# One fused attention and mixture-of-experts kernel: last tiles' ranks from one-hots, an early overflow count, row gathers ahead of weights, an expert's first product in three parts, and a planner's TensorE durations renewed

## The chip, the cores and the metric

The kernel runs on one core of a Trainium2 chip. The metric is the device time of one execution in microseconds (us). The engines are TensorE (PE in the rows; PEld is its loading of stationary operands), VectorE (DVE), ScalarE (ACT), GpSimd (POOL) and SyncE (SP). SP issues most transfers, GpSimd the indirect ones.

## What is computed

```python
# attention: 4 batches, 8 heads, 768 positions of 64, plus 8 memory positions; chunks of 32
for c in range(nc):
    k_full = np.concatenate([mem_k, k_ctx], axis=2)      # 16 left, 32 own, 8 right
    scores = scale * np.matmul(q_c, k_full.transpose(0, 1, 3, 2))
    a = softmax(scores)                                  # + 1e-9 in the denominator
    out[:, :, c_start:c_end] = np.matmul(a, v_full)
# first FFN: 3072 tokens x 512, hidden 2048
h = x @ w_in
x = (h * np.cos(h)) @ w_out
# top-1 of 8 experts (512 -> 1024 -> 512); tokens with x @ w_skip <= 0 keep x
logits = xc @ w_gate
e_idx = np.argmax(logits, axis=1)
h = np.maximum(xc[mask] @ w1[e], 0.0)
y[mask] = gate_w[mask, None] * (h @ w2[e])               # gate_w: the softmax at e_idx
out[do_compute] = xc + y
```

## The kernel before

Every float32 operand of a large product is split into a high and a low part, and a product is the sum of three passes (high by high, high by low, low by high). So one h of a unit is 12 matmuls and one y is 3.

**Stages.** Attention runs over 24 tiles (tile c is chunk c's 32 positions in all four batches, 128 tokens). Two tiles make a group g; the first FFN has 16 pieces of the hidden size, so 192 units (g, f), each with one h (L580, function `plan_unit`), the chain for h cos h on ScalarE and VectorE (L608 to L619), and two y groups (L584). Attention for later tiles lies between the units of earlier ones, so the first FFN begins at 22 us while its weights are still being loaded and unpacked (L546 to L559). A tile whose y is done gets its gate logits: for most tiles on VectorE (L687), for the last two (the tail) as matmuls on TensorE (L782 and L794). `plan_gates` then makes a one-hot of the chosen expert (`onehot`, L716), a rank in the expert's region (`base` L726 and L727: the running count of all tiles before, then `rank` L730 with a triangular matrix), adds the one-hot to the running count (`count`, L722), picks this row's rank (`mine`, L735), adds the offset (`index`, L740) and writes the rows to DRAM at these places (`scatter`, L743, an indirect transfer). A scatter waits until the one before it has landed.

**Experts.** The first expert is named before the tail. After the tail `plan_caps` counts tokens per expert (L844), orders the other seven by size (L848 to L860), and SP loads their seven numbers into registers (L863). From then on SP loads rows of the regions (`plan_rows`, L959, tile xg) and weight pieces (`plan_piece32`, L929, tile raw; converted to w by L238 and L938). The gathers of rows read what the scatters wrote, so they wait for the last scatter. Most experts take `plan_unit2` over two tiles at a time; the first expert and the two small ones (third and seventh in the order) take `plan_pair`, one tile with a quarter of the hidden size: h (L1042, 12 matmuls), relu on ScalarE (L1047), two transposes ("turn", L1052), the split into gh and gl (L238, L1059), two groups of y (L996, 3 matmuls each). `plan_finish` joins (L1084) and puts rows into the output by an indirect transfer (L1088). At the end TensorE counts once more (L1262), VectorE compares with the capacity (L1265 to L1267), all five engines load the result into a register (L1269) and branch on it (L1270); nothing overflows here.

**What sets the order.** A planner on the host (`Schedule`) simulates the engines: each task has an engine, a duration, a key and what it waits for, and whenever an engine comes free it takes the ready task with the smallest key. The instructions are then written in the order the simulation found, and each engine runs its own list strictly in that order. Durations given to the planner thus set the order and nothing else. SP's list is in one order too: a load that waits holds up all loads behind it.

## Time and profile before

| | us |
|---|---|
| runs shown | 853.3, 852.24 (and one of 1259.52) |
| median | 853.3 |
| the profiled execution's own time | 850.34 |
| its span | 848.2 |
| TensorE busy in the span | 820.9 (97%) |
| VectorE, ScalarE, GpSimd busy | 589.9, 525.1, 252.7 |
| granted TensorE clock, mean | 0.995 |

The span runs from the first to the last instruction; 2.1 us of the execution lie around it. Times in rows are us from the span's start. Matmuls are pipelined and their ends are modelled, so that a stretch in which TensorE is shown busy may still hold less work than it could; the start of the next row shows more than a row's length. In the rows of a timeline the bracket at the end gives the idle time before the instruction and what ended it.

### The profile page before, as it was taken

How to read it: one execution, taken by the hardware profiler on the slowest of the kernel's cores; microseconds unless marked ns; L12 is line 12 of the kernel's file. 1: busy time of each engine (PE TensorE's matmuls, PEld its weight loads, DVE VectorE, ACT ScalarE, POOL GpSimd, SP SyncE). 2: the span in 40 equal slices, each digit the busy share in tenths (PEclk: the TensorE clock that was granted, in tenths of full speed). 3: DMA queues.
4: the chain of work that ended last, by engine and by line, in shares of the span. 5: the costliest groups of instructions: out<-in, count | busy, mean ns of one | idle time of the engine just before them, and what ended most of it. 6: DMA issues, size and time to landing. Idle time of an engine off the chain costs nothing.

```text
span 848.2 us, 17771 instructions
## 1 busy us (share of the span) xinstructions
PE 820.9 (97%) x6440; PEld 710.8 (84%) x6440; DVE 589.9 (70%) x1598; ACT 525.1 (62%) x1204; POOL 252.7 (30%) x330
## 2 busy tenths in 40 slices
PE   9899899999999999999999999999999999999994
PEld 4677788778888888888888888888888789889993
DVE  7888874899649376493855839567398386697761
ACT  6887876556657566565665656556577375575551
POOL 6465453323323223232232322323233100010010
PEclk9999999999999999999999999999999999999998
DMA  9469527623123131221312213221213275886640
GB/s 351 165 193 251 179 101 250 182 69 101 44 74 91 33 100 33 85 74 33 100 54 76 71 34 100 65 63 28 104 30 122 86 268 205 277 294 207 204 175 30
DMA packets 37200, 106.08 MB, mean 125 GB/s; under 512 B 6747, under 2 KB 7003, under 8 KB 36976
## 3 DMA queue, kind: packets, MB, share of 16 engines
q1 hardware_dynamic: 34064, 98.74, 38.0%
q0 software_dynamic: 3040, 6.13, 2.0%
q8 instruction: 52, 0.85, 0.4%
q14 instruction: 44, 0.36, 0.1%
HBM read 88.10 MB, written 20.77 MB: 128 GB/s over the span
## 4 chain that ended last, share of the span: by engine, by line
PE 77%; DVE 8%; ACT 5%; issue 3%; DMA 3%; SPq 1%; POOL 1%; DVEq 0%; POOLq 0%; ACTq 0%
PE pb L580 34%; PE py L584 25%; PE py L996 8%; PE pb L448 4%; PE pb L1042 2%; DVE junk L687 2%; PE pb L380 2%; DMA st<-in_w_in_dram 1%; DVE pb L549 1%; DVE cv L555 1%; DVE u L619 1%; DVE ki L608 1%; PE pb L472 1%; DMA raw<-in_w_dram 1%; ACT w L238 1%
## 5 line engine op out<-in xcount | busy, mean ns | idle before, releaser
L580 PE MATMUL pb<-xh,w 128*128 128x256 f32 x1856 | 266.2, 286 | 4.7 <-DVE u L619 3.5
L580 PEld LDWEIGHTS pb<-xh,w 128*128 128x128 f32 x1856 | 246.3, 190 | 27.1 <-DVE u L619 7.0
L627 POOL TENSOR_TENSOR gl<-u,gh 128x256 fp32r<-128x256 f32 x192 | 147.3, 767 | 357.0 <-ACT gh L238 271.3
L584 PE MATMUL py<-w,gh 128*128 128x512 f32 x768 | 244.3, 399 | 0.6 <-ACT yt L238 0.3
L687 DVE SCALAR_TENSOR_TENSOR junk<-yt,wg 128x512 bf16<-128x512 f32 x198 | 149.2, 754 | 7.4 <-ACT yt L238 5.3
L584 PE MATMUL py<-w,gl 128*128 128x512 f32 x384 | 150.8, 393 | 0.8 <-POOL gl L627 0.7
L580 PE MATMUL pb<-xl,w 128*128 128x256 f32 x928 | 148.9, 283 | 0.0
L584 PEld LDWEIGHTS py<-w,gh 128*128 128x128 f32 x768 | 131.8, 190 | 20.3 <-ACT gh L238 1.7
L608 DVE SCALAR_TENSOR_TENSOR ki<-pb,ki 128x256 f32<-128x256 f32 x192 | 80.5, 419 | 82.7 <-ACT ki L238 82.4
L619 DVE SCALAR_TENSOR_TENSOR u<-ki,pb 128x256 f32<-128x256 f32 x192 | 80.0, 417 | 73.6 <-ACT ki L615 70.5
L580 PEld LDWEIGHTS pb<-xl,w 128*128 128x128 f32 x928 | 127.8, 191 | 0.0
L238 ACT ACTIVATE ki<-pb 128x256 int32<-128x256 f32 x192 | 72.9, 381 | 86.7 <-PE pb L580 67.5
L612 ACT ACTIVATE ki<-ki 128x256 f32<-128x256 f32 x192 | 79.7, 416 | 63.5 <-DVE ki L608 63.3
L238 ACT ACTIVATE gh<-u 128x256 fp32r<-128x256 f32 x192 | 79.5, 414 | 57.7 <-DVE u L619 51.0
L938 DVE TENSOR_TENSOR w<-raw,w 128x512 fp32r<-128x512 f32 x128 | 84.4, 693 | 11.8 <-ACT w L238 10.0
L584 PEld LDWEIGHTS py<-w,gl 128*128 128x128 f32 x384 | 72.1, 188 | 20.9 <-POOL gl L627 4.5
L615 ACT ACTIVATE ki<-ki 128x256 f32<-128x256 f32 x192 | 79.7, 415 | 4.7
L238 ACT ACTIVATE w<-raw 128x512 fp32r<-128x512 f32 x128 | 74.8, 625 | 10.4 <-DMA raw<-in_w_dram 9.7
L996 PE MATMUL py<-w,gh 128*128 128x512 f32 x224 | 72.1, 403 | 0.0
L1088 POOL DMA_INDIRECT out_dram<-ot,ri x14 | 14.9, 1062 | 151.9 <-DVE ot L1084 117.9
L559 POOL TENSOR_TENSOR w<-cv,w 128x512 fp32r<-128x512 f32 x32 | 41.3, 1294 | 27.6 <-ACT w L238 26.1
L996 PE MATMUL py<-w,gl 128*128 128x512 f32 x112 | 43.8, 391 | 0.0
(151 smaller groups left out, 840.5 us busy)
## 6 DMA issues: line engine op xcount, KB each, us to landing
raw<-in_w_dram SPq DMA_DIRECT2D x64, 512.0 KB, 4.5
k<-in_kt_dram SPq DMA_DIRECT2D x40, 256.0 KB, 4.9
v<-in_vw_dram SPq DMA_DIRECT2D x40, 256.0 KB, 4.1
st<-in_w_in_dram SPq DMA_DIRECT2D x16, 512.0 KB, 6.5
st<-in_w_out_dram SPq DMA_DIRECT2D x16, 512.0 KB, 3.6
out_dram<-yt SPq DMA_DIRECT2D x96, 64.0 KB, 1.8
q<-in_qt_dram SPq DMA_DIRECT2D x21, 256.0 KB, 2.9
xs<-fl SPq DMA_DIRECT2D x8, 528.0 KB, 11.2
```

The lines of the kernel that those rows point to most:

```text
L238: nc.scalar.activation(out=out, in_=in_, func=AF.Copy, scale=scale)
L559: nc.gpsimd.tensor_tensor(out=wt[f][:, i, 1, :], in0=o["f"], in1=wt[f][:, i, 0, :].bitcast(F32), op=ALU.subtract)
L580: nc.tensor.matmul(ph, w[:, i, ct, :], x[j][:, ct, :], start=(n == 0), stop=(n == len(todo) - 1))
L584: nc.tensor.matmul(py, g[i][:, t * P:t * P + P], w[:, j, :], start=(first and n == 0), stop=(last and n == 2))
L608: nc.vector.scalar_tensor_tensor(out=o["v"], in0=o["p"], scalar=INV2PI / W_SCALE, in1=o["k"], op0=ALU.mult, op1=ALU.subtract)
L612: nc.scalar.activation(out=o["v"], in_=o["v"], func=AF.Sin, scale=math.pi)
L615: nc.scalar.activation(out=o["v"], in_=o["v"], func=AF.Square, scale=math.sqrt(2.0))
L619: nc.vector.scalar_tensor_tensor(out=o["u"], in0=o["v"], scalar=1.0, in1=o["p"], op0=ALU.subtract, op1=ALU.mult)
L627: nc.gpsimd.tensor_tensor(out=o["g"][1], in0=o["u"], in1=o["g"][0].bitcast(F32), op=ALU.subtract)
L687: nc.vector.scalar_tensor_tensor(out=junk, in0=o["y"][:, 0:DM], scalar=1.0, in1=state["wg"][:, j, :], op0=ALU.mult, op1=ALU.mult, accum_ou ...
L938: nc.vector.tensor_tensor(out=part(s, 1), in0=half(s), in1=part(s, 0).bitcast(F32), op=ALU.subtract)
L996: nc.tensor.matmul(ey[p, t], g[i][:, cols], w[:, j, 512 * (f % 2):512 * (f % 2) + 512], start=(f == 0 and q == 0), stop=(f == n - 1 and q ...
```

## The change

1. The planner's durations of seven TensorE tasks are set anew: transposes of attention and splits 0.87 to 0.45, scores and weighted sums 0.95 to 0.69, the tail's transposes and dots to 0.45, h 1.32 to 1.44, y 0.66 to 0.69.
2. `plan_pair`: h is planned as three tasks of four matmuls, so that other TensorE work may stand between them.
3. The tail: the second tile's base takes the first one's one-hot as a matmul of its own, and the counts are three matmuls over the running count and the two one-hots. The two `count` additions of the tail are gone.
4. Row gathers have the key of their use less GK = 8, where it was less 2; weight pieces keep less 2.
5. The overflow number is worked out on VectorE right behind `caps` (`most`), from a copy of the counts. The matmul and four VectorE instructions at the end are gone; the load into registers stays.

```diff
+GK = 8
@@ plan_xt, plan_chunk, plan_tail_logits (the last two of these lines)
-        a = pe(0.87, key, pe_x, after + [xt], new=[b], use=use)
+        a = pe(0.45, key, pe_x, after + [xt], new=[b], use=use)
-        t = pe(0.95, key, scores, [lq] + lk + s0 + clean["k", z], new=[b1] + mine, use=[sq, sk] + bz(0) + bz(2) + hold)
+        t = pe(0.69, key, scores, [lq] + lk + s0 + clean["k", z], new=[b1] + mine, use=[sq, sk] + bz(0) + bz(2) + hold)
...
@@ plan_unit
-        t = pe(1.32, i - AHEAD * end, h, [w_ready["i", f]] + xt_ready[g], new=[b], use=[w_slot[f], xt_slot[g]])
+        t = pe(1.44, i - AHEAD * end, h, [w_ready["i", f]] + xt_ready[g], new=[b], use=[w_slot[f], xt_slot[g]])
...
@@ plan_gates
         def base():
             o["r"] = bank()[:, 0:E]
+            if tail:
+                end_hots.setdefault("sum", state["sum"])
+                end_hots[t] = o
             nc.tensor.matmul(o["r"], ones, first_slot, start=True, stop=False)
             nc.tensor.matmul(o["r"], ones, state["sum"], start=False, stop=False)
+            if tail and t:
+                nc.tensor.matmul(o["r"], ones, end_hots[0]["oh"], start=False, stop=False)
...
-        if c == NCH - 2:
-            before = [last["skip"]]
+        if tail:
+            before = [last["skip"]] + ([last["hot"]] if t else [])
...
-        n = dve(0.07, key + 0.01, count, [h, r])
+        if tail:
+            n = last["hot"] = r
+        else:
+            n = dve(0.07, key + 0.01, count, [h, r])
@@ plan_counts
-            nc.tensor.matmul(o["p"], ones, state["sum"], start=True, stop=True)
+            terms = [end_hots["sum"], end_hots[0]["oh"], end_hots[1]["oh"]] if first else [state["sum"]]
+            for n, x in enumerate(terms):
+                nc.tensor.matmul(o["p"], ones, x, start=(n == 0), stop=(n == len(terms) - 1))
...
             if first:
+                state["cnt"] = sm.tile([P, E], F32, name="cnt")
+                nc.vector.tensor_copy(out=state["cnt"], in_=o["p"])
@@ plan_caps
+        def most():
...
+            nc.vector.tensor_tensor(out=state["over"], in0=state["cnt"], in1=state["cp"], op=ALU.subtract)
+            nc.vector.reduce_max(out=top, in_=state["over"], axis=AX.X)
+            nc.vector.tensor_copy(out=state["top"], in_=top)
+
+        x = dve(0.07, key + 9, caps, [o["sort"]])
+        dve(0.25, key + 9.5, most, [x])
@@ plan_rows
-        x = load(key - 2, ld, P * ROW * 4, [last["reg", p]] + after, new=[s_xg])
+        x = load(key - GK, ld, P * ROW * 4, [last["reg", p]] + after, new=[s_xg])
@@ plan_pair
-        def h():
-            o["p"] = bank()[:, 0:G]
+        def h(third):
+            if not third:
+                o["p"] = bank()[:, 0:G]
...
-        x = pe(1.32, key, h, w2_ready[ma] + xt_ready["x", p][t:t + 1], new=[b1],
+        x = pe(0.48, key, lambda: h(0), w2_ready[ma] + xt_ready["x", p][t:t + 1], new=[b1],
                use=[w2_slot[ma], xt_slot["x", p]])
+        for third in (1, 2):
+            x = pe(0.48, key, lambda third=third: h(third), [x], use=[b1, w2_slot[ma], xt_slot["x", p]])
@@ the end
-    nc.tensor.matmul(pc, ones, state["sum"], start=True, stop=True)
-    nc.vector.tensor_copy(out=cnt, in_=pc)
...
-    nc.vector.tensor_copy(out=topi, in_=top)
     order_cm.__exit__(None, None, None)
-    most = nc.values_load(topi[0:1, 0:1], min_val=0, max_val=NT + P)
+    most = nc.values_load(state["top"][0:1, 0:1], min_val=0, max_val=NT + P)
```

**First place: TensorE at the beginning of the first FFN.** Before (names: k0, k1 and q0, more are keys and queries of a chunk, xh and xl the first group's input, w_112 the first weight piece):

```order
L315 MATMUL pb_405<-ones_83 64x512
L448 MATMUL py_409<-k0_96,q0_98 32x128 x16
L580 MATMUL pb_430<-xh_108,w_112 128x256 x8
L580 MATMUL pb_430<-xl_109,w_112 128x256 x4
L448 MATMUL py_453<-k1_101,more_103 32x128 x16
L580 MATMUL pb_476<-xh_108,w_113 128x256 x8
```

In the changed kernel, on the same engine at the same place (a row of L316 is a filler matmul, which no result uses):

```order
L316 MATMUL pb_398<-ones_83 64x512
L581 MATMUL pb_401<-xh_108,w_112 128x256 x8
L581 MATMUL pb_401<-xl_109,w_112 128x256 x4
L449 MATMUL py_418<-k0_96,q0_98 32x128 x16
L316 MATMUL pb_439<-ones_83 64x512
```

The first h now stands ahead of the scores that preceded it. From here to the row at which 180.6 us is reached in the profile, TensorE's list holds the same tasks in another order, less two fillers; the scores of the next two tiles, for one, stand one and two y groups earlier. From 180.6 to about 640 us the list is the same task by task.

**Second place: SP's queue and TensorE behind the scatters.** SP before, behind the seven register loads (only the transfers; the register arithmetic between them is left out):

```order
L959 DMA xg_9356<-xs_80 128x528
L929 DMA raw_9361<-in_w12_dram 128x1024
L929 DMA raw_9366<-in_w12_dram 128x1024
L959 DMA xg_9370<-xs_80 128x528
L959 DMA xg_9375<-xs_80 128x528
L929 DMA raw_9380<-in_w12_dram 128x1024
```

SP in the changed kernel:

```order
L981 DMA xg_9342<-xs_80 128x528
L981 DMA xg_9347<-xs_80 128x528
L981 DMA xg_9355<-xs_80 128x528
L951 DMA raw_9362<-in_w12_dram 128x1024
L951 DMA raw_9367<-in_w12_dram 128x1024
```

The three gathers stand together ahead of all weight pieces. Behind fourteen transfers stands SP's load of the overflow number, which was the last thing in its list. On TensorE the first split of gathered rows (L380) stood behind all four h of the first tile and seven of its eight y groups:

```order
L996 MATMUL py_9227<-w_8824,gl_9354 128x512
L380 MATMUL pb_9390<-cb_81,xg_9356 128x128 x4
L996 MATMUL py_9227<-w_8824,gh_9353 128x512 x2
L996 MATMUL py_9227<-w_8824,gl_9354 128x512
L1042 MATMUL pb_9409<-w_8523,xh_9021 128x256 x4
```

Now it stands behind four of the eight, and the next two splits follow with one y group between (L381 splits, L1018 y):

```order
L381 MATMUL pb_9380<-cb_81,xg_9342 128x128 x4
L1018 MATMUL py_9301<-w_8769,gh_9352 128x512 x2
L1018 MATMUL py_9301<-w_8769,gl_9353 128x512
L381 MATMUL pb_9408<-cb_81,xg_9347 128x128 x4
L1018 MATMUL py_9301<-w_8769,gh_9352 128x512 x2
L1018 MATMUL py_9301<-w_8769,gl_9353 128x512
L381 MATMUL pb_9428<-cb_81,xg_9355 128x128 x4
```

Three y groups moved from ahead of the first split to behind it, and the two fillers that stood ahead of it are gone from here.

**Third place: TensorE at the end.** Before, the last h (L1042), the last turn (L1052) and what stands behind:

```order
L1042 MATMUL pb_11310<-w_10944,xh_10942 128x256 x4
L996 MATMUL py_11292<-w_10872,gh_11296 128x512 x2
L996 MATMUL py_11292<-w_10872,gl_11297 128x512
L1052 MATMUL pb_11328<-cb_81,u_11326 128x128 x2
L996 MATMUL py_11292<-w_10872,gh_11296 128x512 x2
L996 MATMUL py_11292<-w_10872,gl_11297 128x512
L996 MATMUL py_11292<-w_10932,gh_11306 128x512 x2
```

Five y groups begin behind the turn (the last row here is the second of them); the first three do not need this turn. Now:

```order
L1018 MATMUL py_11288<-w_10939,gl_11320 128x512
L1066 MATMUL pb_11323<-w_10951,xh_10949 128x256 x4
L1076 MATMUL pb_11344<-cb_81,u_11342 128x128 x2
L1018 MATMUL py_11288<-w_11002,gh_11347 128x512 x2
L1018 MATMUL py_11288<-w_11002,gl_11348 128x512
L1018 MATMUL py_11288<-w_11002,gh_11347 128x512 x2
L1018 MATMUL py_11288<-w_11002,gl_11348 128x512
```

No y group stands between the last third of h and its turn, and only the two that need this turn stand behind it.

## Rows read from the trace of the kernel before

**Rows 1.** Windows view: stretch, length, busy us of PE, PEld, DVE, ACT, POOL; clock; DMA.

```profile
22.40:160.00 137.60, 130.30 (x1038) 109.37 (x1038) 104.79 (x208) 105.53 (x238) 68.80 (x77) 1.00 0.63 191
160.00:181.00 21.00, 18.21 (x169) 14.27 (x171) 20.83 (x74) 11.30 (x23) 5.94 (x8) 1.00 0.37 95
181.00:663.00 482.00, 481.10 (x3947) 424.46 (x3938) 325.81 (x994) 296.90 (x697) 146.16 (x211) 1.00 0.25 69
663.00:691.00 28.00, 25.84 (x171) 21.32 (x171) 16.70 (x65) 15.10 (x38) 2.97 (x3) 1.00 0.59 213
691.00:836.00 145.00, 144.96 (x935) 130.61 (x933) 102.68 (x225) 80.99 (x189) 12.92 (x12) 1.00 0.62 210
836.00:848.20 12.20, 0.22 (x2) 0.10 (x1) 1.30 (x5) 0.00 (x0) 0.98 (x1) 0.68 0.09 28
```

**Rows 2.** Lines view of TensorE in 22.4 to 180.6: busy, mean ns, idle before it.

```profile
L580 PE MATMUL pb<-xh,w 128*128 128x256 f32 x352 | 51.4, 289 | 4.7 <-DVE u L619 3.5 <-DVE cv L555 1.1
```

**Rows 3.** Timeline of TensorE around the first h: start, length, engine, line, instruction.

```profile
22.36 1.08 PE L448 MATMUL py<-k,q 128*32 128x128 f32 x32
23.38 0.85 PE L580 MATMUL pb<-xh,w 128*128 128x256 f32 x5
```

**Rows 4.** Timeline of SyncE's queue at 63 us, the loads of one chunk's keys.

```profile
63.35 1.11 SPq L417 DMA_DIRECT2D k<-in_kt_dram  x2
```

**Rows 5.** DMA view of 60 to 70 us: issues, KB each, median us to landing.

```profile
k<-in_kt_dram SPq DMA_DIRECT2D x2, 256.0 KB, 9.2
```

**Rows 6.** Timeline of TensorE, scores of that chunk.

```profile
81.20 1.08 PE L448 MATMUL pb<-k,more 128*32 128x128 f32 x32
```

**Rows 7.** Timeline of GpSimd, the two last scatters.

```profile
666.22 1.01 POOL L743 DMA_INDIRECT xs<-yt,si  x1 [6.94 <-ACT u L1047]
670.52 0.98 POOL L743 DMA_INDIRECT xs<-yt,si  x1 [3.29 <-DVE gl L1059]
```

**Rows 8.** Timeline of VectorE, the second scatter's row numbers.

```profile
667.17 0.16 DVE L740 TENSOR_TENSOR si<-sl,aw 128x1 int32<-128x1 f32 x1
```

**Rows 9.** Timeline of SyncE's queue behind the scatters.

```profile
674.09 0.37 SPq L959 DMA_DIRECT2D xg<-xs  x1
...
675.79 0.87 SPq L959 DMA_DIRECT2D xg<-xs  x2
```

**Rows 10.** Timeline of TensorE between the FFN and the second expert.

```profile
673.31 0.40 PE L315 MATMUL pb<-ones 128*64 128x512 bf16 x1
673.64 0.74 PE L996 MATMUL py<-w,gh 128*128 128x512 f32 x2
...
677.31 0.63 PE L380 MATMUL pb<-cb,xg 128*128 128x128 f32 x4 [0.76 <-DMA xg<-xs]
...
681.87 1.28 PE L380 MATMUL pb<-cb,xg 128*128 128x128 f32 x8 [1.31 <-DMA xg<-xs]
```

**Rows 11.** Timeline of ScalarE, one conversion of a weight half.

```profile
684.97 0.63 ACT L238 ACTIVATE w<-raw 128x512 fp32r<-128x512 f32 x1
```

**Rows 12.** Timeline of TensorE and ScalarE, last tile.

```profile
831.15 0.64 PE L1042 MATMUL pb<-w,xh 128*128 128x256 f32 x4
...
832.33 0.44 PE L1052 MATMUL pb<-cb,u 128*128 128x128 f32 x2
...
832.80 0.38 ACT L238 ACTIVATE gh<-pb 128x256 fp32r<-128x256 f32 x1 [0.53 <-PE pb L1052]
...
833.31 0.62 PE L996 MATMUL py<-w,gh 128*128 128x512 f32 x2
...
834.00 0.61 PE L996 MATMUL py<-w,gh 128*128 128x512 f32 x2
```

**Rows 13.** Timeline of VectorE and GpSimd, the end.

```profile
836.24 0.75 DVE L1084 SCALAR_TENSOR_TENSOR ot<-py,gs,xg 128x512 f32<-128x512 f32 x1 [2.60 <-PE pb L1262]
...
837.27 0.98 POOL L1088 DMA_INDIRECT out_dram<-ot,ri  x1 [6.77 <-DVE over L1265]
```

**Rows 14.** Instructions of line 1269 on GpSimd's queue.

```profile
L1269 POOLq TENSOR_LOAD <-topi x1: 503/503/503, 837.7 to 837.7; - x1
```

More of the change, by code (lines that the diff above doesn't have):

```diff
@@ L498, in rest @@
             r = dve(0.12, key, lambda: nc.vector.reciprocal(out=o["r"], in_=o["r"]), [r])
-            t = pe(0.87, key + step, pe_t, [e, t_cb], new=[b2], use=[ss] + hold)
+            t = pe(0.45, key + step, pe_t, [e, t_cb], new=[b2], use=[ss] + hold)
             t = act(0.48, key + step, lambda: copy(s(), o["p"]), [t, r0], use=[b2, ss] + hold)
-            t = pe(0.95, key + 2 * step, pv, [t] + lv + clean["v", z], new=[b3], use=[sv, ss] + bz(1) + hold)
+            t = pe(0.69, key + 2 * step, pv, [t] + lv + clean["v", z], new=[b3], use=[sv, ss] + bz(1) + hold)
             t = dve(0.6, key + 3 * step, norm, [t, r], use=[b3, ss] + hold)
@@ L647, in plan_unit @@
             own = [y_slot[g][n]]
-            y_last[g, n] = pe(0.66, i + YK + (SKEW * n if end else 0.1 * n), lambda n=n: y(n),
+            y_last[g, n] = pe(0.69, i + YK + (SKEW * n if end else 0.1 * n), lambda n=n: y(n),
                               [t, w_ready["o", f]] + prev, new=own if not f else [],
                               use=(own if f else []) + [w_slot[f], s_g])
-    wg_ready, picks, scattered = [], {}, []
+    wg_ready, picks, scattered, end_hots = [], {}, [], {}
     def plan_gates(c, key, dkey, tail):
@@ L794, in dots @@
                 nc.tensor.matmul(o["q"], yT()[:, ct, :], wgt[:, ct, :], start=(ct == 0), stop=(ct == NCT - 1))
-        x = pe(0.87, key, pe_y, [ev], new=[b1], use=[s_yt])
+        x = pe(0.45, key, pe_y, [ev], new=[b1], use=[s_yt])
         x = (dve if t else act)(0.5, key, out_y, [x, last["yT"]], use=[b1, xt_slot["tail"]])
-        x = pe(0.85, key, dots, [x], new=[b2], use=[xt_slot["tail"]])
+        x = pe(0.45, key, dots, [x], new=[b2], use=[xt_slot["tail"]])
         o["bank"] = b2
@@ L915, in caps @@
                                     scalar2=float(P - CAP), op0=ALU.is_le, op1=ALU.mult)
-        dve(0.07, key + 9, caps, [o["sort"]])
+        def most():
+            state["over"] = sm.tile([P, E], F32, name="over")
+            state["top"] = sm.tile([P, 1], I32, name="topi")
+            top = sm.tile([P, 1], F32, name="top")
+            nc.vector.tensor_tensor(out=state["over"], in0=state["cnt"], in1=state["cp"], op=ALU.subtract)
[3 more added lines that the diff above has]
+        dve(0.25, key + 9.5, most, [x])
     def plan_piece32(m, key):
@@ L1017, in plan_unit2 @@
         end = p == E - 1 and f >= NF2 - 4
[L1018 removed]
+        x = pe(1.44, key, h, w2_ready[ma] + xt_ready["x", p], new=[b], use=[w2_slot[ma], xt_slot["x", p]])
         w2_used[ma] = w2_used.get(ma, x)
@@ L1024, in plan_unit2 @@
             own = [] if f else [open_y(p, t)]
-            ey_last[p, t] = pe(0.66, key + 1.6 + (10 * t if end else 0.1 * t),
+            ey_last[p, t] = pe(0.69, key + 1.6 + (10 * t if end else 0.1 * t),
                                lambda t=t: mm_y2(p, t, o["g"], slice(t * P, t * P + P), wt["x", mb], f, NF2),
@@ L1035, in plan_pair @@
         b1, b2, s_u, s_g = slot("b"), slot("b"), slot("u"), slot("g")
-        def h():
-            o["p"] = bank()[:, 0:G]
+        def h(third):
+            if not third:
+                o["p"] = bank()[:, 0:G]
             wv = wt["x", ma].rearrange("p s (c f) -> p s c f", c=NCT)
             x = xT["x", p]
-            for n, (i, k, ct) in enumerate((i, k, ct) for i, k in PASSES for ct in range(NCT)):
+            i, k = PASSES[third]
+            for ct in range(NCT):
                 nc.tensor.matmul(o["p"], x[k][:, ct, t * P:t * P + P], wv[:, i, ct, :],
-                                 start=(n == 0), stop=(n == 3 * NCT - 1))
+                                 start=(third + ct == 0), stop=(third == 2 and ct == NCT - 1))
         def relu():
@@ L1070, in plan_pair @@
             own = [] if f else [open_y(p, t)]
-            ey_last[p, t] = pe(0.66, key + 1.6 + 0.1 * i,
+            ey_last[p, t] = pe(0.69, key + 1.6 + 0.1 * i,
                                lambda i=i, f=f: mm_y2(p, t, o["g"], slice(i * P, i * P + P), wt["x", mb], f, NF2),
@@ L1255, in one_tile @@
         )
-    cnt = sm.tile([P, E], F32, name="cnt")
-    top = sm.tile([P, 1], F32, name="top")
-    topi = sm.tile([P, 1], I32, name="topi")
-    pc = bank()[:, 0:E]
-    nc.tensor.matmul(pc, ones, state["sum"], start=True, stop=True)
-    nc.vector.tensor_copy(out=cnt, in_=pc)
-    over = sm.tile([P, E], F32, name="over")
-    nc.vector.tensor_tensor(out=over, in0=cnt, in1=state["cp"], op=ALU.subtract)
-    nc.vector.reduce_max(out=top, in_=over, axis=AX.X)
-    nc.vector.tensor_copy(out=topi, in_=top)
     order_cm.__exit__(None, None, None)
-    most = nc.values_load(topi[0:1, 0:1], min_val=0, max_val=NT + P)
+    most = nc.values_load(state["top"][0:1, 0:1], min_val=0, max_val=NT + P)
     with tc.If(most > CAP):
         with tc.tile_pool(name="ov", bufs=1) as ov:
-            more_tiles(ov, cnt, over)
+            more_tiles(ov, state["cnt"], state["over"])
 def _windows(x, mem):
```

1 line of the change is left out of this document (removed).

## The prediction

> **What bounds the kernel now.** I read the windows view first, cut at the borders of the stages. From 181 to 663 us TensorE is busy for 481.1 of 482.0 us, and from 691 to 836 us for 144.96 of 145; the granted clock is 1.00 in all stretches before 836, the upper of its two levels (2.4 GHz) [rows 1]. Nothing off TensorE can be seen to cost there. What can be gained or lost lies in three places: the lead-in, 22.4 to 181 us, where the first FFN runs while attention and the unpacking of weights go on (7.3 + 2.8 = 10.1 us idle); the transition to the experts, 663 to 691 us (2.2 us idle, and two fillers, which are no work); and the end behind 836 us, where TensorE has 0.22 us to do in 12.2 [rows 1].
>
> Next the lines view of the lead-in: h waits there for the two steps on VectorE that make its input free or its weights ready (3.5 and 1.1 us) [rows 2]. VectorE is busy for 20.83 of 21 us from 160 to 181, and for 104.8 of 137.6 before [rows 1]. So the last part of the lead-in is VectorE's, and its 2.8 idle us on TensorE don't go away by another order on TensorE.
>
> Then the timelines of the two other places. In the transition a chain binds that TensorE has no part in. The second scatter's row numbers are there at 667.17 + 0.16 = 667.3 [rows 8], but it starts at 670.52, since the first, begun at 666.22, has to land: 4.3 us between them [rows 7]. The first gather starts at 674.09, 3.57 us behind the second scatter [rows 7, 9], and its rows reach TensorE at 677.31, 3.22 us later [rows 10]. At the end TensorE runs out at 836.2, and the last join (836.24), the last put (837.27) and the branch follow one another [rows 13, 14].
>
> **The change, part by part.** All is worked out against the profiled execution, 850.34 us. The runs shown are 852.24 and 853.3 beside it; I take the middle one of 850.34, 852.24 and 853.3 for the kernel before, 1.9 above the profile's.
>
> *Durations.* They change nothing but the order, and by the lists only before 181 us and after about 640. In the lead-in the first h now stands ahead of the scores that preceded it, which took 23.38 − 22.36 = 1.02 us [rows 3]: the first FFN can start 1.0 us earlier. Some splits ahead of it also moved forward, so that it may be 2. Further on the lists are level to within one or two y groups, and what paces TensorE is VectorE. I take −1.5 us. The bounds: nothing better than all 7.3 idle us before 160; on the other side, the scores of the next tiles come one or two y groups (0.69 us each, 834.00 − 833.31 [rows 12]) and the start's 1.0 to 2.0 us earlier, and their keys might be late. I looked at that: the keys of the chunk scored at 81.20 [rows 6] are loaded from 63.35 to 64.46 [rows 4] and land 9.2 us after issue [rows 5], at 73.7 at the latest. 81.20 − 1.4 − 2.0 = 77.8 is still 4 us behind. A loss can come from a unit whose y was put ahead of its gh, at most about as much as the idle time that h now has to VectorE, 3.5 us. So −7.3 to +3.5.
>
> A rule speaks for more than this. The steady stretch has weight loading busy for 424.46 of 482 us, 0.881; the lead-in has 123.64 of 158.6, 0.780 [rows 1]. At the steady density its loads would need 140.4 us, so that 18.2 us could be had, not 10.1. The Trainium skill (Perfetto Trace Analysis, Identifying the Most-Contended Engine) says that matmul busy time is a bad measure of how close TensorE is to its limit and that the busy share of weight loading is a better one; the two figures of this trace differ in its sense. By the rule an order that closed half of the gap would bring 9 us, by the idle time half of 10.1, 5.
>
> *One-hots.* They take two additions on VectorE (0.16 us each, as the step at 667.17 [rows 8]) out of the chain of ranks and add three 8-column matmuls. The first scatter's numbers come some 0.3 us earlier. As the second waits for the first to land, not for its numbers, only the 0.3 is passed on: the gathers start at about 673.8.
>
> *Gathers.* Before, the second and third gather went out at 675.79 [rows 9], behind two weight pieces, and TensorE waited for them at 681.87 (1.31 us); for the first it waited 0.76 us at 677.31 [rows 10]. Now all three go out in a row at 673.8 and land from 673.8 + 3.22 = 677.0 on. But TensorE's list has moved too: three y groups, 2.07 us, and two fillers, 2 × 0.33 us (673.64 − 673.31 [rows 10]), no longer stand ahead of the first split. It is reached at 677.31 − 0.76 − 2.07 − 0.66 = 673.8 and waits 3.2 us. The two others land in the shadow of the first and its y group. Before: 0.76 + 1.31 + 0.66 = 2.73 us without work; now 3.2. I take +0.5. Bounds: −2.7 if the wait shrinks to nothing, +2.1 if the weight pieces, issued some 1.2 us later behind three gathers instead of one, make h wait as long as the splits did (2.07).
>
> *Thirds.* The parts cost nothing in themselves, they are the same twelve matmuls. What they change is what covers the chain from h to y. At the end: the last four matmuls of h were issued from 831.15, 0.12 us each, so until 831.63, and the turn began at 832.33, 0.70 later, behind one y group and 0.27 us of idle time. gh was ready at 832.80 + 0.38 = 833.18, that is 0.66 us after the turn's two matmuls (832.33 + 0.19) [rows 12]; three y groups that did not need it covered that. Now nothing stands in either gap: 0.70 + 0.66 = 1.36 us idle where 0.27 was, +1.1 us. This I hold for nearly certain; bounds +0.8 to +1.5. In the fifteen other pairs at least 0.68 us of other work stands in the first gap and at least 1.17 in the second: covered, if ScalarE is free.
>
> *Overflow number.* One 8-column matmul and four short VectorE instructions are gone from behind the last y. The register load on GpSimd's queue was at 837.7 and took 0.50 us [rows 14], after the put's start at 837.27; without the wait for VectorE it can stand right behind the put's issue. I take −0.4 us; bounds 0 (the put alone holds the branch) and −1.0 (join and put start earlier as well). SyncE now loads that number in the middle of its list; by then VectorE has long written it, and the load takes as long as one of the seven before.
>
> The sum: −1.5 + 0.5 + 1.1 − 0.4 = −0.3 us. In the profile's terms 850.0, in those of the runs 852.24 − 0.3 = **851.9 us**.
>
> **The rivals.**
>
> *The lead-in closes.* For it: 10.1 idle us and a density of 0.780 against 0.881. Against it: VectorE's 104.8 of 137.6 and 20.83 of 21 us [rows 1], and that the list differs by little beyond the first ten units. If it closes a third of the 18.2 us: −6, so 852.24 − 6 − 1.5 + 2.7 = about **847**. Closing all 18 would be faster by over 2%.
>
> *The change doesn't do what it says.* The renewed order gains nothing, since VectorE paces the lead-in, and the gathers in front gain nothing, since the scatters hold them. Then only the last pair and the branch show: 852.24 + 0.5 + 1.1 − 0.4 = **853.4**. For it: the 4.3 us between the scatters, and h waiting for VectorE [rows 2, 7].
>
> *Slower: the thirds leave turns uncovered.* Place: ScalarE's relu behind the last third. Nine of the sixteen turns now have only 0.68 to 0.69 us of TensorE's other work ahead of them, counted in the list, where five had so little; that just equals the 0.70 from h to turn. ScalarE runs in order, and a weight conversion takes 0.63 us [rows 11]; where one stands ahead of relu, the turn waits by that much. It decides from one conversion on. At eight turns, 8 × 0.63 = 5.0: 851.9 + 5.0 = **856.9**. Against it: five turns were as bare before, and TensorE lost 0.04 us in 145 [rows 1].
>
> **How the numbers follow.** My forecast, 849 to 853 without the rivals' mechanisms, has 0.48; a lead-in that closes 0.19; no effect but the end's 0.19; uncovered turns 0.14. The range 846 to 857.5 leaves out about a third of the first rival and half of the slower one, 0.13 in all. A measurement of this kernel can tell about 2%, 17 us, from no change. Below 835 lies only a lead-in that closes entirely, 0.02; above 869 only eight or more turns that wait with both of their gaps, and more that I don't see, 0.02; so within 2%: 0.96.
>
> **What would show it.** In the lead-in: the first h at 21.4 to 22.4 us, and the task that stood at 181 at 178 to 180. If it stands at 175, the first rival is right, and windows show weight loading above 0.80. In the transition: the gathers issued together at about 673.8 less what the lead-in gained, one wait of TensorE for xg of about 3 us in place of 0.76 and 1.31, none for the second and third. If the wait is under 1 us, my chain of scatters is wrong. In the experts: waits of turns for relu add to under 1 us before the last; over 3 would be the slower rival. At the end: two gaps on TensorE around the last turn, of 0.5 to 0.75 us each, and the branch about 0.4 us sooner behind the put. The forecast is wrong if TensorE's list takes another time between 181 and 640 us, where it is the same in both: then something that I hold for equal, such as the clock, is not.

## Result and profile after

The changed kernel takes 857.88 us (median of 7 runs), the kernel before 854.0; the ratio is 1.0052, 95% interval [1.0031, 1.0073], so +4.4 us [+2.6, +6.2]; one run of the kernel before, of 1259.52 us, is left out of the ratio. I had forecast 851.9 and a range that ends at 857.5. Of the 6.0 us between forecast and result, 1.8 are the kernel before, which I had taken at 852.24; the rest is the change. The profiled execution took 855.48 us, with a span of 853.6 us: 5.4 more than before.

The windows of the changed kernel, cut as before (columns as in [rows 1]; the last one ends with the longer span):

```profile
22.40:160.00 137.60, 129.76 (x1046) 107.32 (x1046) 105.35 (x209) 106.32 (x235) 70.74 (x77) 1.00 0.65 194
160.00:181.00 21.00, 19.75 (x155) 16.53 (x158) 20.86 (x75) 11.60 (x27) 7.62 (x9) 1.00 0.31 83
181.00:663.00 482.00, 478.60 (x3914) 419.45 (x3907) 330.88 (x985) 291.61 (x692) 138.11 (x206) 1.00 0.25 68
663.00:691.00 28.00, 24.89 (x173) 21.07 (x172) 14.81 (x67) 13.21 (x33) 3.20 (x7) 1.00 0.47 160
691.00:836.00 145.00, 144.75 (x937) 130.45 (x936) 107.24 (x230) 84.87 (x195) 13.47 (x13) 1.00 0.63 222
836.00:853.60 17.60, 6.99 (x38) 5.15 (x36) 1.71 (x4) 1.53 (x4) 0.97 (x1) 0.82 0.07 21
```

The stretch in which I had expected nothing, 181 to 663 us, has lost 2.5 us of TensorE's busy time (478.60 of 482, where 481.10 had been) and more of its weight loading (419.45, where 424.46 had been) [rows 1]. The lead-in's last part is better than before (19.75 of 21 us for 18.21). How far the work has come at a time is seen better at fixed instructions than in busy times. The rank matmuls of the changed kernel (timeline of TensorE, one per tile, five of 24):

```profile
179.17 0.17 PE L736 MATMUL pb<-oh,tri 128*128 128x8 bf16 x1 [0.88 <-DVE oh L717]
...
189.69 0.17 PE L736 MATMUL pb<-oh,tri 128*128 128x8 bf16 x1
...
601.70 0.18 PE L736 MATMUL pb<-oh,tri 128*128 128x8 bf16 x1
...
646.03 0.18 PE L736 MATMUL pb<-oh,tri 128*128 128x8 bf16 x1
...
670.94 0.18 PE L736 MATMUL pb<-oh,tri 128*128 128x8 bf16 x1
```

In the trace of before the same five stand at 179.70, 189.35, 598.09, 640.12 and 664.85 us; three of them:

```profile
189.35 0.18 PE L730 MATMUL pb<-oh,tri 128*128 128x8 bf16 x1
...
598.09 0.18 PE L730 MATMUL pb<-oh,tri 128*128 128x8 bf16 x1
...
664.85 0.18 PE L730 MATMUL pb<-oh,tri 128*128 128x8 bf16 x1
```

With the splits, puts and the end beside them, changed less before:

| place in the program | changed, us | changed less before, us |
|---|---|---|
| first h | 22.41 | -0.97 |
| rank, end of the lead-in | 179.17 | -0.53 |
| rank, next tile | 189.69 | +0.34 |
| rank, near the end of the steady stretch | 601.70 | +3.61 |
| rank, tail of the first FFN | 646.03 | +5.91 |
| rank of the first tail tile | 670.94 | +6.09 |
| first split of gathered rows | 682.13 | +4.82 |
| put, middle experts (before at 719.53) | 725.24 | +5.71 |
| put, middle experts (before at 809.65) | 815.93 | +6.28 |
| last put | 845.06 | +7.79 |
| end of the span | 853.6 | +5.4 |

So 5.75 us go between 189 and 665 us, where I had expected no change; 0.4 come back by 719, 0.6 go in the third expert, 1.5 in the last, and 2.4 come back behind the last put. What TensorE waited for in the changed kernel (waits view: total, times, longest):

```profile
PE py L585 <- POOL gl L628: 2.2, 3, 1.0
PE pb L1076 <- ACT u L1071: 1.7, 2, 1.1
PE pb L381 <- DMA xg<-xs: 1.6, 1, 1.6
...
PE pb L904 <- DVE osum L723: 1.2, 1, 1.2
```

None of these waits lies in the steady stretch, though it lost 3.3 us; only those for osum and one for gl (1.0 us) lie in its tail. The waits for the gathers are 1.6 us in one, where they were 0.76 and 1.31 [rows 10].

**Theories.** A: the renewed durations moved VectorE's list too. TensorE's list is the same from 181 to about 630 us, VectorE's isn't: once in each group of two tiles, before, VectorE's list reads (with the two VectorE steps of h cos h called ki and u) u, dot, ki, then the softmax's maximum; now u, dot, dot, ki, maximum. The second dot is the first gate dot of the next tile, which stands one h step too early; what follows shifts. In ScalarE's list two steps of each group change places with a neighbour, which is a rival to VectorE's list within A. B: the loss is from the thirds and the regrouped gathers, by waits in the experts. C: the chip or its clock was slower in these runs.

### The profile page after: what moved, and what is told of

Its sections match the earlier page's. It is cut to its first block, busy times and chain, and to the rows that moved or that the text cites. A ratio compares the mean times of both kernels' runs of the same rounds, so it can differ in the third digit from the quotient of the medians.

```text
span 853.6 us, 17769 instructions
## 1 busy us (share of the span) xinstructions
PE 824.6 (97%) x6442; PEld 710.6 (83%) x6442; DVE 596.9 (70%) x1596; ACT 523.0 (61%) x1204; POOL 247.3 (29%) x330
## 4 chain that ended last, share of the span: by engine, by line
PE 61%; DVE 22%; issue 6%; DMA 4%; ACT 4%; POOL 1%; SPq 0%; DVEq 0%; POOLq 0%; ACTq 0%
PE pb L581 26%; PE py L585 18%; DVE junk L688 11%; PE py L1018 8%; PE pb L449 3%; DVE u L620 2%; DVE ki L609 2%; PE pb L1066 2%; DMA raw<-in_w_dram 2%; PE pb L381 2%; DMA st<-in_w_in_dram 1%; DVE r L468 1%; PE pb L316 1%; DVE w L960 1%; PE py L449 1%
## 5 line engine op out<-in xcount | busy, mean ns | idle before, releaser
L688 DVE SCALAR_TENSOR_TENSOR junk<-yt,wg 128x512 bf16<-128x512 f32 x198 | 154.2, 779 | 6.6 <-ACT yt L239 4.2
L1018 PE MATMUL py<-w,gh 128*128 128x512 f32 x224 | 71.8, 402 | 0.5 <-ACT gh L239 0.5
L1018 PE MATMUL py<-w,gl 128*128 128x512 f32 x112 | 44.0, 393 | 0.2 <-DVE gl L1036 0.2
```

What stands on the lines that cost most here:

```text
L688: nc.vector.scalar_tensor_tensor(out=junk, in0=o["y"][:, 0:DM], scalar=1.0, in1=state["wg"][:, j, :], op0=ALU.mult, op1=ALU.mult, accum_ou ...
L1018: nc.tensor.matmul(ey[p, t], g[i][:, cols], w[:, j, 512 * (f % 2):512 * (f % 2) + 512], start=(f == 0 and q == 0), stop=(f == n - 1 and q ...
```

## Experiments

The edits are against the kernel named; ratios are to the kernel before, on the same chip.

**Renewed durations alone**

```diff
 kernel before, all seven durations
-        a = pe(0.87, key, pe_x, ...
+        a = pe(0.45, key, pe_x, ...
-        t = pe(1.32, i - AHEAD * end, h, ...
+        t = pe(1.44, i - AHEAD * end, h, ...
```

> The kernel before with the renewed TensorE durations alone (h of a pair 1.44 in one piece). Theory A, VectorE's list: the durations move one gate dot per tile ahead of the softmax and of h's next step on VectorE, though TensorE's list stays the same between 181 and 640 us. Then this kernel carries nearly the whole loss: about +0.43 us per 52 us group from 190 to 600 us and some 6 us by 660 us, so 6 to 8 us more than before (nothing here gives the 2.4 us back at the end). Rival B, the experts: the loss comes from the thirds and the regrouped gathers, and the durations are worth nothing by themselves: within 1.5 us of before. Rival C, the chip or the clock was slower in the runs of the changed kernel: within 1.5 us, and the steady stretch keeps step with before.

859.55 us, ratio 1.0093 [1.0066, 1.0120]: +7.9 us, more than the whole change costs, as A had it (6 to 8). Rank by rank it runs in step with the changed kernel (from +1.50 at 190 us to +4.77 at 598 and +7.06 at 640). B and C fall; the other four parts together bring about 3.5 us.

**The changed kernel with the old durations**

```diff
 changed kernel
-        a = pe(0.45, key, pe_x, ...
+        a = pe(0.87, key, pe_x, ...
-        x = pe(0.48, key, lambda: h(0), ...
+        x = pe(0.44, key, lambda: h(0), ...
```

> The changed kernel with the durations of before (a third of a pair's h 0.44). Theory A: TensorE and VectorE keep step with before up to 600 us; what is left is the early count (-2.4), the transition (about -1) and the thirds (+2): 0 to 2.5 us less than before, 5 to 7 less than the changed kernel. Rival B, the experts: as slow as the changed kernel, 3 to 5 us more than before.

849.61 us, ratio 0.9972 [0.9951, 0.9992]: 2.4 us less than before and, by the ratios, 6.8 less than the changed kernel, both inside what A had. All ranks up to 640 us stand at -0.1 us against before.

**VectorE's list alone, in the steady stretch.** The planner is run twice on copies, once with the old and once with the new durations; then TensorE's, ScalarE's and GpSimd's tasks are chained in the old order, VectorE's between units 48 and 160 (`sc.keep(48, 160)`) in the new one. Nothing else is planned anew, and the three other lists come out as in the kernel before.

```diff
 kernel before
...
+        mine, theirs = self.twin_order(False), self.twin_order(True)
...
+        for eng in ('PE', 'ACT', 'Pool') + ('DVE',):
+            chain = [n for n in mine if T[n].eng == eng]
+            if eng in ('DVE',):
+                moved = [n for n in theirs[cut(theirs, lo):cut(theirs, hi)] if T[n].eng == eng]
+                seen = set(moved)
+                at = next(i for i, n in enumerate(chain) if n in seen)
+                chain = chain[:at] + moved + [n for n in chain[at:] if n not in seen]
+            for a, b in zip(chain, chain[1:]):
+                self.link(T[a], T[b])
...
+    sc.keep(48, 160)
```

> The kernel before, with TensorE's, ScalarE's and GpSimd's lists unchanged; only VectorE's list between units 48 and 160 of the first FFN (about 197 to 530 us) is the one that the renewed durations give: in each group of two tiles the second tile's first gate dot stands one h step earlier, and what follows it shifts by one. Theory A, the dot: +0.43 us per group over some 6 to 7 groups, +2.5 to +3.1 us, in steps of 0.43 at the place in each group where h then waits for its bank. Rival: the steady loss of the changed kernel comes from ScalarE's or GpSimd's list or from where things lie in memory: 0 us, no steps.

The chains shift the planner's own clock a little, and ten of SyncE's transfers changed places, so a control was run with the same chains, VectorE's in the old order too. Its lists differ from the moved-dots kernel's by VectorE's alone.

```diff
 kernel with moved dots
-        for eng in ('PE', 'ACT', 'Pool') + ('DVE',):
+        for eng in ('PE', 'ACT', 'Pool', 'DVE') + ():
...
-            if eng in ('DVE',):
+            if eng in ():
```

> The control to the kernel with the moved dots: all of its lists (SyncE's ten moved transfers too), but VectorE's as before. In the moved-dots kernel the lead-in was 2.4 us late with a 3.2 us wait of h and a granted clock of 0.57 right behind it. Theory A: the dots cost 2.97 us there and the rest is SyncE's ten transfers: the control shows the same late lead-in and the long wait, no steps between 197 and 530 us, and is 2 to 4 us faster than the moved-dots kernel, 2 to 4 slower than before. Rival: the lists are not what matters, but the way the planner is held: as slow as the moved-dots kernel.

Moved dots: 860.2 us, ratio 1.0092 [1.0061, 1.0122]; control: 857.18 us, 1.0033 [1.0017, 1.0049]. By the ratios they are 5.0 us apart, where I had expected 2 to 4; the intervals leave about 3 us on either side, so the step is read from the profiles. Ranks of the control (timeline of TensorE):

```profile
206.44 0.18 PE L760 MATMUL pb<-oh,tri 128*128 128x8 bf16 x1
...
550.44 0.18 PE L760 MATMUL pb<-oh,tri 128*128 128x8 bf16 x1
...
669.57 0.23 PE L760 MATMUL pb<-oh,tri 128*128 128x8 bf16 x1
```

and of the kernel with moved dots at 204.55, 236.91, 289.34 and 551.52 (in the control 206.44, 238.44, 290.44 and 550.44):

```profile
204.55 0.18 PE L760 MATMUL pb<-oh,tri 128*128 128x8 bf16 x1
...
236.91 0.18 PE L760 MATMUL pb<-oh,tri 128*128 128x8 bf16 x1
...
289.34 0.18 PE L760 MATMUL pb<-oh,tri 128*128 128x8 bf16 x1
...
551.52 0.18 PE L760 MATMUL pb<-oh,tri 128*128 128x8 bf16 x1
```

They are 1.89 us ahead of the control at the first (in their lead-in the clock was low for about half as long, see the last section), 1.53 at the second, 1.10 at the third, and 1.08 behind at the last: 2.97 us lost in 345 us, in seven steps of 0.36 to 0.44, one per group. Expected were 2.5 to 3.1. The control has no such steps: from 206 to 550 us its ranks keep one offset to the kernel before. How a step comes about is seen in the timelines of VectorE and TensorE around one of them. The control:

```profile
274.42 0.41 DVE L649 SCALAR_TENSOR_TENSOR u<-ki,pb 128x256 f32<-128x256 f32 x1
...
274.62 1.08 PE L478 MATMUL pb<-v,sa 128*32 128x128 f32 x32
...
275.63 1.22 PE L610 MATMUL pb<-xh,w 128*128 128x256 f32 x8
```

The moved dots:

```profile
274.07 0.42 DVE L649 SCALAR_TENSOR_TENSOR u<-ki,pb 128x256 f32<-128x256 f32 x1
...
273.35 1.08 PE L478 MATMUL pb<-v,sa 128*32 128x128 f32 x32
...
274.54 1.21 PE L610 MATMUL pb<-xh,w 128*128 128x256 f32 x8
```

The offset here is -1.53 us, so that u, which reads the last of a bank of h (pb) and so frees it, would stand at 272.89; it stands at 274.07, since VectorE has done one dot more by here and is 1.2 us late. That dot took 1.17 us:

```profile
263.93 1.17 DVE L717 SCALAR_TENSOR_TENSOR junk<-yt,wg 128x512 bf16<-128x512 f32 x1
```

The moved dot takes 1.16 to 1.17 us in every group, here and in the changed kernel, where the median of all dots is 0.69. In this row GpSimd's gl runs beside it for 0.62 us; whether that is what makes it long was not tried. In the control the next h starts as soon as the attention's weighted sum is issued (1.01 us behind its start). With moved dots it starts 1.19 us behind it, when u has ended (274.07 + 0.42): 0.18 us. The h ahead of it starts 0.16 us late in the same sense (271.73, in the control 273.10), and the weighted sum behind that another 0.10; together that is the step. That h waits for u is in the trace (the semaphore that it waits for is the one u raises), but no view lists it as a wait: the weighted sum is shown busy until 274.43, and the 0.11 us left are too short for a bracket. The busy share doesn't show it either: from 181 to 530 us TensorE is busy for 347.93 us with moved dots and for 348.34 in the control, 0.4 us apart; weight loading is busy for 304.38 and 306.87, 2.5 apart. The Trainium skill (Perfetto Trace Analysis, Identifying the Most-Contended Engine) calls the busy share of matmuls a poor measure of how close TensorE is to its limit and that of weight loading a better one; these two runs agree: by 530 us moved dots have lost 2.5 us (1.89 ahead at the first rank, 0.64 behind at the one that stands at 531.20 in the control).

**VectorE's list alone, in the tail of the first FFN**

```diff
 kernel with moved dots
-    sc.keep(48, 160)
+    sc.keep(160, 187)
```

> The same with only the stretch of units 160 to 187 (about 530 to 650 us) of VectorE's list as the renewed durations give it, up to the last tiles on which VectorE does dots. Theory A: the loss between 530 and 660 us, where VectorE is fully busy: +2 to +3.5 us by the last put. Rival: that loss comes from TensorE's own list, which differs from 640 us on: under +1 us.

858.59 us, ratio 1.0062 [1.0040, 1.0084]. Two ranks (the control's stand above at 550.44 and 669.57):

```profile
550.48 0.18 PE L760 MATMUL pb<-oh,tri 128*128 128x8 bf16 x1
...
673.34 0.23 PE L760 MATMUL pb<-oh,tri 128*128 128x8 bf16 x1
```

0.04 us behind the control at the first, 3.77 at the second: 3.7 us by VectorE's list alone. At the last put, where I had expected +2 to +3.5, the profiles are 1.9 us apart (847.02 and 845.15), since the control's clock fell once more at 689 us; by the ratios the kernel is 2.5 us slower than the control. The longest of it is TensorE's wait for the running count, osum, which VectorE writes (waits view, control first):

```profile
PE pb L921 <- DVE osum L752: 0.7, 1, 0.7
```

```profile
PE pb L921 <- DVE osum L752: 2.3, 1, 2.3
```

The two stretches make 6.7 us; the changed kernel lost 5.75 there. In its tail TensorE's list differs too, which I didn't take apart.

**Early count alone**

```diff
 kernel before
+        dve(0.25, key + 9.5, most, [x])         # over, reduce, cast, behind caps
-    nc.tensor.matmul(pc, ones, state["sum"], start=True, stop=True)   # and four VectorE steps, at the end
```

> The kernel before with the overflow number worked out behind caps, all else as before. The trace of the changed kernel has 8.54 us from the last put's start to the end of the span, before had 10.93. Theory A: that is the early count's doing, since four engines can take the branch before the last join: 1.8 to 2.6 us less than before. By my prediction: 0.4 us less, bounds 0 and 1.0. Rival: the 2.4 us come from something else (where the last instructions of the engines lie): no change.

851.56 us, ratio 0.9994 [0.9981, 1.0007]: -0.5 us [-1.6, +0.6]. That holds my forecast of -0.4 and leaves out the 1.8 to 2.6 that A had here. In the profile the stretch from the last put's start to the end of the span is 9.15 us, where before had 10.93. Over all kernels run here it is 8.39 to 10.12 us in the seven with the early count and 10.57 to 11.05 in the seven without. So the profiles show some 1.8 us gained in this stretch, and the medians less than that; why they differ stays open.

**Thirds alone**

```diff
 kernel before
-        x = pe(1.32, key, h, ...
+        x = pe(0.48, key, lambda: h(0), ...
+        for third in (1, 2):
+            x = pe(0.48, key, lambda third=third: h(third), [x], ...
```

> The kernel before with h of a pair in three parts, all else as before. From the joins of the changed kernel: +0.6 us over the third expert, +1.5 over the last. Theory A: 1 to 2.5 us more than before, the two gaps around the last turn (0.7 us each) among them. Rival B: +4 or more, with waits for relu at many turns. A third way: the parts help in the transition by as much as they cost at the end, no change.

854.7 us, ratio 1.0026 [1.0004, 1.0047]: +2.2 us, inside the 1 to 2.5 expected. From the put before at 809.65 to the last one it loses 1.5 us, as the changed kernel does.

**Gathers ahead alone**

```diff
 kernel before
+GK = 8
...
-        x = load(key - 2, ld, P * ROW * 4, ...
+        x = load(key - GK, ld, P * ROW * 4, ...
```

> The kernel before with the gathers' key less 8 alone. My prediction's step says that the scatters hold the gathers, so that they go out at the same time, and TensorE waits for the first alone: -1.3 to +2.1 us, about 0. Rival: three gathers at once land later than one, all of TensorE's first splits wait, and weight pieces behind them are late: +2 or more, with the granted clock falling behind the wait.

854.77 us, ratio 1.0025 [1.0004, 1.0047]: +2.1 us, at the upper end of what I had allowed and at the lower end of the rival's +2; the runs don't tell the two apart. The clock did not fall behind these waits, as the rival had it: in this profile it fell at 92 and 665 us. The profile has a wait of 2.3 us for gathered rows and one of 2.2 us of a turn for relu; before, the longest for rows was 1.31 [rows 10]. That relu is late because ScalarE converts weight pieces, which now come behind three gathers, fits but wasn't tried by itself.

**The changed kernel with old durations and h in one piece**

```diff
 changed kernel, old durations
-        x = pe(0.44, key, lambda: h(0), ...
+        x = pe(1.32, key, h, ...
```

> The changed kernel with the durations of before and h of a pair in one piece: what is left is the one-hots, the gathers ahead and the early count. With the parts as seen so far (early count -1.8 at the end, thirds +2 taken out of a kernel at 849.6): 2 to 4.5 us less than before, and 1 to 2 less than the changed kernel with old durations. Rival: the thirds help the transition by filling its waits, and without them the gain is smaller than that kernel's 2.4: between -2 and 0.

852.64 us, ratio 0.9991 [0.9974, 1.0008]. With thirds it was 0.9972. That is -0.8 us, not the 2 to 4.5 that adding up the parts gave, and what the rival had. So the thirds, which cost 2.2 us alone, cost nothing beside gathers ahead and may help; the intervals overlap.

**Renewed durations in the lead-in only, without thirds**

```diff
 kernel with h in one piece
-        t = pe(1.32, i - AHEAD * end, h, ...
+        t = pe(1.44 if i < 44 else 1.32, ...
-        t = pe(0.95, key, scores, ...
+        t = pe(0.69 if key < 44 else 0.95, ...
```

> The kernel without thirds and, up to unit 44 alone (180 us), the renewed durations; from there on all four engines' lists are as with the old ones. The lead-in was 0.5 us ahead at 180 us in the changed kernel and 0.6 behind in the kernel with durations alone. Theory A: within 1 us of the kernel without thirds. My prediction's step (-1.5, bounds -7.3 and +3.5) would have it 1.5 us faster.

850.72 us, ratio 0.9956 [0.9937, 0.9975], beside 0.9991 [0.9974, 1.0008] without them in the same series: the medians differ by 1.9 us, the intervals just touch. The steady stretch keeps step (all ranks from 190 to 640 us at one offset).

**The whole change, renewed durations in the lead-in only**

```diff
 changed kernel
-        t = pe(1.44, i - AHEAD * end, h, ...
+        t = pe(1.44 if i < 44 else 1.32, ...
```

> The whole changed kernel, but the renewed durations only up to unit 44 (180 us); behind that all lists of the first FFN are as before. Theory A, VectorE's list: the 3 us of the steady stretch and 3 us of its tail are gone: 5 to 8 us less than the changed kernel, 1.5 to 4 us less than before. Rival B, the experts: as slow as the changed kernel, +3 to +5.

850.43 us, ratio 0.9968 [0.9954, 0.9983]: 2.7 us less than before and about 7 less than the changed kernel, as A had it. This and the kernel of the section before are faster than the kernel before and the changed kernel; which of the two is better the intervals don't tell.

**The same, last h in one piece**

```diff
 kernel before it
+        last_one = p == E - 1 and j == NF2 // 2 - 1
-        for third in (1, 2):
+        for third in () if last_one else (1, 2):
```

> The same with h of the very last pair planned and issued in one piece, so that four y groups stand behind the last turn again before its own two. The two gaps of 0.7 us around the last turn should be gone: 1.0 to 1.6 us less than the kernel with all thirds, if the gaps are what costs there; no change if the branch on the overflow number, not the last join, sets the end.

851.73 us, ratio 0.9979 [0.9961, 0.9996]: no gain, where I had expected 1.0 to 1.6 us if the gaps cost there. The kernel that it was to mend doesn't have the gaps; its last turn (timeline of TensorE) is followed by a y group at once:

```profile
833.43 0.44 PE L1076 MATMUL pb<-cb,u 128*128 128x128 f32 x2
...
833.62 0.71 PE L1018 MATMUL py<-w,gh 128*128 128x512 f32 x2
```

With old durations for this part the planner put one y group behind the last turn that doesn't need it. The thirds of 0.48 us alone, with the other durations old, have them (the run of thirds alone: 0.69 and 0.72 us, one filler in the first), so the renewed durations are not needed for them. With 0.44 us for a third, gathers ahead and the early count they are gone; which of these takes them away was not tried.

## Why the prediction was wrong

**The step that failed** is the one on the durations: "They change nothing but the order, and by the lists only before 181 us and after about 640." I had compared TensorE's lists and said it of all. VectorE's list changed in every group, and its cost there, 2.97 us with all else held, and 3.7 us in the tail, is the whole loss and more. The sentence that TensorE is busy for 481.1 of 482 us, "Nothing off TensorE can be seen to cost there" [rows 1], was right for the order of before, and taken as if it held for any order: h's bank came free just in time, and one dot more ahead of u, of 1.17 us at its place, was enough. None of my rivals had this. The one on the slower side put its 5 us in relu behind weight conversions; turns waited 1.7 us in the changed kernel, not 5, so that its 856.9 lies near the result by chance. The sign that I had named came: for the stretch that took from 189.35 to 598.09 us before, the changed kernel takes 3.27 us more, with the same list on TensorE, and 5.57 to the rank at 640.12. What was not equal is VectorE's list, not the clock, which is 1.00 there in both. And I had misread [rows 2]: u, for which h waits 3.5 us in the lead-in, frees the bank that h writes, not its input. That wait decided here.

Why a truer duration makes a worse order is argued, not shown: with h at 1.44 us the planner sees VectorE free a little sooner than the next step of h is ready, and takes the next task by key, a dot. On VectorE that dot takes 1.17 us, where the planner has 0.62.

**Lead-in, -1.5.** The first h came 0.97 us earlier, as [rows 3] had it. 0.53 us were left at 179 us, and at 190 the changed kernel was 0.34 behind. By the profiles the term is about 0; by the two kernels that differ in it, -1.9 us with intervals that touch. Two more kernels differ in it alone, both with thirds (old durations, 0.9972, and renewed ones in the lead-in only, 0.9968), and there it is -0.3. It stays open between 0 and -1.9. The keys were not late, and the lead-in did not close.

**One-hots.** They were not run alone. The first scatter stands 1.47 us behind the rank of the first tail tile (672.41 and 670.94) where it stood 1.37 behind: the 0.3 us don't show there.

**Transition, +0.5.** From the tail's rank (+6.09) to the middle experts (+5.71) 0.4 us came back. Two sizes of the chain were off, both taken too long, and a wait came that I had not in the sum (timelines of GpSimd, SyncE and TensorE, changed kernel):

```profile
672.41 1.01 POOL L749 DMA_INDIRECT xs<-yt,si  x1 [6.57 <-DVE si L746]
...
675.88 0.98 POOL L749 DMA_INDIRECT xs<-yt,si  x1 [2.46 <-DVE gl L1083]
678.93 1.51 SPq L981 DMA_DIRECT2D xg<-xs  x3
682.13 0.63 PE L381 MATMUL pb<-cb,xg 128*128 128x128 f32 x4 [1.64 <-DMA xg<-xs]
...
690.40 0.44 PE L1076 MATMUL pb<-cb,u 128*128 128x128 f32 x2 [1.12 <-ACT u L1071]
```

The second scatter starts 3.47 us behind the first, not 4.3, and the gathers 3.05 behind the second, not 3.57 [rows 7, 9]; so the one wait that I had at 3.2 us was 1.6. The turn then waited 1.12 us for relu; my upper bound had a wait of this kind, for h. That the gathers ahead cost 2.1 us [+0.3, +4.0] when they are alone suggests that this term hangs on what else is moved.

**Thirds, +1.1.** +1.5 over the last expert, of which the two gaps I named are 0.68 and 0.72 us (by their issue, the last four matmuls of h take until 840.74, the turn's two until 841.61; timeline of the end):

```profile
840.26 0.63 PE L1066 MATMUL pb<-w,xh 128*128 128x256 f32 x4
...
841.42 0.44 PE L1076 MATMUL pb<-cb,u 128*128 128x128 f32 x2 [0.53 <-ACT u L1071]
...
842.33 0.73 PE L1018 MATMUL py<-w,gh 128*128 128x512 f32 x2 [0.47 <-ACT gh L239]
...
845.06 0.97 POOL L1114 DMA_INDIRECT out_dram<-ot,ri  x1 [9.45 <-DVE ot L1110]
```

My sum had 0.27 us of idle time ahead of this turn before; the y group there fills 0.69 of the 0.70 us, so that the same rows give 1.36 - 0.01 = 1.35, beside the 1.40 here. The third expert lost another 0.6 us, which I had not foreseen; I didn't take it apart.

**Overflow number, -0.4.** -2.4 in this profile, beyond my bound of -1.0; by the medians of the early count alone -0.5, as forecast. I had counted the wait for the load only, and from the put's start to GpSimd's branch 0.6 us are gone (0.9 before, 838.2 - 837.27; 0.3 now, 845.4 - 845.06). Before, all five engines branch between 838.2 and 838.3 us, and GpSimd goes on at 842.8, 4.6 us later (instructions of the branch's line):

```profile
L1270 POOLq EVENT_SEMAPHORE  x5: 17/43/43, 842.8 to 843.2; - x5
...
L1270 POOLq COMPARE_BRANCH  x1: 53/53/53, 838.2 to 838.2; - x1
```

In the changed kernel they come one by one:

```profile
L1286 SPq EVENT_SEMAPHORE  x9: 17/17/17, 826.5 to 827.1; - x9
L1286 POOLq EVENT_SEMAPHORE  x5: 17/43/43, 848.2 to 848.6; - x5
...
L1286 SPq COMPARE_BRANCH  x1: 53/53/53, 822.0 to 822.0; - x1
L1286 ACTq COMPARE_BRANCH  x1: 50/50/50, 842.4 to 842.4; - x1
...
L1286 POOLq COMPARE_BRANCH  x1: 53/53/53, 845.4 to 845.4; - x1
```

GpSimd branches at 845.4 and goes on at 848.2, 2.8 us later. With the early count alone it is 3.4:

```profile
L1271 POOLq EVENT_SEMAPHORE  x5: 17/43/43, 841.1 to 841.4; - x5
...
L1271 POOLq COMPARE_BRANCH  x1: 53/53/53, 837.7 to 837.7; - x1
```

So the larger part of what the profiles show gained is in GpSimd's branch itself. The Trainium skill (Runtime: NRT & Kernel Launch, Instruction fetch mechanics) says that a taken branch to a place that isn't fetched yet waits for a transfer of instructions. A wait of this kind agrees with the rows, which don't tell it from another. Why GpSimd's is shorter now is not shown: that five branches together slow each other would fit it, but SyncE, which branches alone at 822.0, goes on at 826.5, 4.5 us later.

One number of the rivals: in the sum for the lead-in that closes, the 2.7 has no row. With -6 in the place of -1.5, the three other terms give +1.2 and the same 847.

## What to carry to other kernels

Where a planner makes the lists of several engines, a new duration for one engine is a new order for all: compare every engine's list, above all in the stretches where the one that binds keeps its own. An engine that is off the path by its busy share still sets the time through the order of its list, by when it frees the banks of the one that binds. And compare kernels at the same instruction, not by matmul busy time or shown waits: 3 us spread over 345 show in neither.

## What the runs showed of the hardware

Runs of the kernel before lie 6 to 8 us apart within a series, and the slower ones mostly have the lower mean granted clock (between 0.996 and 0.988). In several of the profiles the clock falls to its lower level for a few microseconds behind a standstill of TensorE. In the control, in the lead-in (timeline, then one window: length, busy times, clock, DMA):

```profile
93.19 2.08 PE L610 MATMUL pb<-xh,w 128*128 128x256 f32 x8 [3.23 <-DVE u L649]
```

```profile
92.00:94.00 2.00, 0.81 (x4) 0.82 (x5) 0.75 (x2) 2.00 (x7) 0.22 (x1) 0.52 0.03 10
```

TensorE stood for 3.2 us, and the clock was at about 0.5 from 92 to about 99 us, a loss of some 3 us on top of the wait. It fell also behind standstills of 2.0 us (gathers ahead, at 91.4 us, and renewed durations in the lead-in, at 83.7), but not behind one of 2.03 us in the profile of before, at the place of the first of these (91.2), so that a standstill of this length may or may not cost it. In eight of the fourteen profiles it also fell between 663 and 673 us, right behind the tail's gate logits on TensorE, where no standstill is over 0.2 us; in before, with the same work there, it didn't. In the changed kernel with old durations TensorE stood 3.2 us for relu (waits view), and the clock was low from 1 us before its end to about 6 us behind it:

```profile
PE pb L1076 <- ACT u L1071: 3.2, 1, 3.2
```

Such falls are a part of why single profiles here differ by 3 us and more where the medians don't, and why this document reads steps between two instructions of one profile, and medians for whole kernels.
